# Engine orders from a list schedule, four shared PSUM slots, 1/x from its own activation table, and half-tile silu in a codec kernel

## Chip, cores, metric

One core of one Trainium2 chip. The metric is the device time of one execution in microseconds, lower is better; "median" is the median of the runs of one kernel. Engines: PE (matmul), DVE (VectorE), ACT (ScalarE), POOL (GpSimd), SP (issues the input DMAs).

## The reference

x is [2, 16000, 512] in bf16. A three-tap filter along time and a silu, four stages of residual quantization with a codebook of eight vectors each, and a three-tap filter over the chosen vectors:

```
z = silu(sum_i xp[:, i:i+T, :] * dw_enc[i])          # 3 taps, xp padded in time
res, q = z, 0
for s in range(4):
    d2  = |res|^2 - 2 * res . codebooks[s] + |codebooks[s]|^2
    sel = codebooks[s][argmin(d2)]
    q, res = q + sel, res - sel
y = sum_i qp[:, i:i+T, :] * dw_dec[i]                # 3 taps, qp padded in time
```

## The kernel before

A tile is 14 groups of 128 rows (1792 columns per channel block of 128 channels; there are four such blocks). A tile passes through *front* (taps and silu on DVE and ACT), *select* (products with the codebooks on PE, then a chain of small DVE steps that picks the vectors of stages 0 to 2), *resid* (24 updates of z through PSUM, then stage 3), and *back* (decode on PE, copies on ACT, store). Eighteen tiles, several in flight. The program only emits the steps in a rough order; the framework's own scheduler then orders each engine's instructions.

```python
psA = ctx.enter_context(tc.tile_pool(name="psA", bufs=3, space=bass.MemoryType.PSUM))  # 2 banks each
psS = ctx.enter_context(tc.tile_pool(name="psS", bufs=2, space=bass.MemoryType.PSUM))  # 1 bank each
...
def taps(st, i):                      # one channel block
    for k in range(K):
        t = ppool.tile([P, R], BF16, name=f"P{k}")
        nc.vector.tensor_scalar(out=t, in0=X[:, i, k:k + G, :]..., scalar1=WENC[:, i, k:k + 1], ... op0=ALU.mult)
    nc.vector.tensor_tensor(out=pk[0], in0=pk[0], in1=pk[1], op=ALU.add)
    nc.vector.tensor_tensor(out=pk[0], in0=pk[0], in1=pk[2], op=ALU.add)
    nc.scalar.activation(pk[1], pk[0], ACT.Exp, scale=-1.0)
def plus1(st, i):
    nc.vector.tensor_scalar(out=pk[1], in0=pk[1], scalar1=1.0, scalar2=None, op0=ALU.add)
    nc.scalar.activation(LN, pk[1], ACT.Ln)                    # 1/x = exp(-ln x), one table set
    nc.scalar.activation(pk[1], LN, ACT.Exp, scale=-1.0)
def gate(st, i): ...                  # z = tap sum * 1/(1 + exp(-tap sum))
...
def decide(st, s):                    # each step needs the result of the one before
    ... RC = pC + S; TR = cast(rr); PR = RC - CCF
    V = PR + TR; KEY = V + CCB; M = min(KEY); OH = (KEY == M)
def correct(st, s):                   # OT = copy of transposed OH; E2 = RC * OH; RD = sum(E2); rr += RD; pC = matmul
...
for _, _, f in sorted(order, key=lambda t: t[:2]):
    f()
```

Of the kernel before, what the change touches and what calls it, by code (L numbers as in the profile page):

```python
# [8 lines left out]
BF16 = mybir.dt.bfloat16  # L9
# [6 lines left out]

@with_exitstack
def kernel(
# [8 lines left out]





# [7 lines left out]
    G = 14  # L39
    GH = G // 2  # L40
    GC = G * C
    R = G * P
# [3 lines left out]
    assert T >= R  # L46
# [5 lines left out]
    ppool = ctx.enter_context(tc.tile_pool(name="ppool", bufs=3))  # L52
    lpool = ctx.enter_context(tc.tile_pool(name="lpool", bufs=2))
    selp = ctx.enter_context(tc.tile_pool(name="selp", bufs=2))
    small = ctx.enter_context(tc.tile_pool(name="small", bufs=3))
    ypool = ctx.enter_context(tc.tile_pool(name="ypool", bufs=2))
    psA = ctx.enter_context(tc.tile_pool(name="psA", bufs=3, space=bass.MemoryType.PSUM))
    psS = ctx.enter_context(tc.tile_pool(name="psS", bufs=2, space=bass.MemoryType.PSUM))


    nc.scalar.preload_act_table_set("natural_log_exp_and_others")


    IDENT = const.tile([P, P], BF16, name="IDENT")
    make_identity(nc, IDENT)
    ONES = const.tile([P, P], BF16, name="ONES")
    nc.vector.memset(ONES, 1.0)

    BIG = float(2.0 ** 100)
    MSK = const.tile([P, 3, ZW], BF16, name="MSK")  # L70
    nc.gpsimd.memset(MSK, 0.0)
    for u in range(3):
        nc.vector.tensor_scalar(out=MSK[:, u, N3:N3 + P], in0=IDENT, scalar1=BIG, scalar2=-BIG,
                                op0=ALU.mult, op1=ALU.add)

    WENC_b = const.tile([P, KT, K], BF16, name="WENC_b")
    WDBC = const.tile([P, K, D], BF16, name="WDBC")

    CB4 = const.tile([P, D], BF16, name="CB4")
    CB1 = const.tile([NC, D], BF16, name="CB1")  # L80
    wd_rows = bass.AP(tensor=dw_dec.tensor, offset=dw_dec.offset, ap=[[0, P], [D, K], [1, D]])
    with nc.allow_non_contiguous_dma(reason="small weights"):
        for k in range(K):
            nc.scalar.dma_start(out=WENC_b[:, :, k], in_=dw_enc[k].rearrange("(i p) -> p i", p=P))
        nc.scalar.dma_start(out=CB1, in_=codebooks.flatten_outer_dims())
        for s in range(Nq):
            for j in range(4):
                nc.scalar.dma_start(out=CB4[NC * s + C * j:NC * s + C * (j + 1), :], in_=codebooks[s])
        nc.scalar.dma_start(out=WDBC, in_=wd_rows)
    WENC = const.tile([P, KT, K], F32, name="WENC")  # L90
    nc.vector.tensor_copy(WENC, WENC_b)


    CBT = const.tile([P, KT, NC], BF16, name="CBT")
    CBM2 = const.tile([P, KT, NC], BF16, name="CBM2")
    for i in range(KT):
        pt = psS.tile([P, 512], F32, name="pt", tag="pss")
        ptb = pt.bitcast(BF16)[:, 0:NC]
        nc.tensor.transpose(ptb, CB1[:, i * P:(i + 1) * P], IDENT[0:NC, 0:NC])
        nc.vector.tensor_copy(CBT[:, i, :], ptb)  # L100
        nc.vector.tensor_scalar(out=CBM2[:, i, :], in0=ptb, scalar1=-2.0, scalar2=None, op0=ALU.mult)


    NZ = 3
    ZB = [const.tile([P, KT, G, ZW], BF16, name=f"ZB{b}") for b in range(NZ)]
    for b in range(NZ):
        for i in range(KT):
            nc.vector.tensor_copy(ZB[b][:, i, :, 0:N3], CBM2[:, i:i + 1, 0:N3].to_broadcast([P, G, N3]))
            nc.vector.tensor_copy(ZB[b][:, i, :, N3 + P:ZW], CBM2[:, i:i + 1, N3:NC].to_broadcast([P, G, C]))


    NX = 2
    XT = [const.tile([P, KT, G + 2, P], BF16, name=f"XT{b}") for b in range(NX)]
    for b in range(NX):
        nc.gpsimd.memset(XT[b][:, :, 0, 0:2], 0.0)
        nc.gpsimd.memset(XT[b][:, :, G + 1, P - 2:P], 0.0)


    pg = psS.tile([P, 512], F32, name="pg", tag="pss")
    for i in range(KT):  # L120
        nc.tensor.matmul(pg[0:NC, 0:NC], lhsT=CBT[:, i, :], rhs=CBT[:, i, :],
                         start=(i == 0), stop=(i == KT - 1))
    GR = const.tile([NC, NC], F32, name="GR")
    nc.vector.tensor_copy(GR, pg[0:NC, 0:NC])
    NPART = 3
    GP = const.tile([NC, NPART, NC], BF16, name="GP")
    GREM = const.tile([NC, NC], F32, name="GREM")
    nc.vector.tensor_copy(GP[:, 0, :], GR)
    nc.vector.tensor_tensor(out=GREM, in0=GR, in1=GP[:, 0, :], op=ALU.subtract)
    nc.vector.tensor_copy(GP[:, 1, :], GREM)  # L130
    nc.vector.tensor_tensor(out=GREM, in0=GREM, in1=GP[:, 1, :], op=ALU.subtract)
    nc.vector.tensor_copy(GP[:, 2, :], GREM)


    CCF = const.tile([P, 1, NC], F32, name="CCF")
    CCB = const.tile([P, 1, NC], BF16, name="CCB")
    CCD = const.tile([NC, NPART, NC], BF16, name="CCD")
    nc.vector.tensor_tensor(out=CCD, in0=GP, in1=IDENT[0:NC, 0:NC].rearrange("p (o c) -> p o c", o=1).to_broadcast([NC, NPART, NC]),
                            op=ALU.mult)
    pc = psS.tile([P, 512], F32, name="pc", tag="pss")  # L140
    for q in range(NPART):
        nc.tensor.matmul(pc[:, 0:NC], lhsT=ONES[0:NC, :], rhs=CCD[:, q, :], start=(q == 0), stop=(q == NPART - 1))
    nc.vector.tensor_copy(CCF[:, 0, :], pc[:, 0:NC])
    nc.vector.tensor_copy(CCB[:, 0, :], pc[:, 0:NC])



    GM = const.tile([GC, G, 1], F32, name="GM")
    nc.vector.tensor_reduce(out=GM[:, :, 0], in_=IDENT[0:GC, 0:GC].rearrange("p (g c) -> p g c", c=C), axis=AX.X, op=ALU.add)
    BD = {}  # L150
    for s in range(2):
        SEL = const.tile([NC, G, C], BF16, name=f"SEL{s}")
        nc.vector.tensor_copy(SEL, IDENT[0:NC, s * C:(s + 1) * C].rearrange("p (o c) -> p o c", o=1).to_broadcast([NC, G, C]))
        RP = const.tile([GC, NPART, NC], F32, name=f"RP{s}")
        pr = psS.tile([P, 512], F32, name="pr", tag="pss")
        nc.tensor.matmul(pr[0:GC, 0:NPART * NC], lhsT=SEL.rearrange("p g c -> p (g c)"),
                         rhs=GP.rearrange("p q c -> p (q c)"), start=True, stop=True)
        nc.vector.tensor_scalar(out=RP.rearrange("p q c -> p (q c)"), in0=pr[0:GC, 0:NPART * NC], scalar1=2.0,
                                scalar2=None, op0=ALU.mult)
        for s2 in range(s + 1, 3):  # L160
            for q in range(NPART):
                t = const.tile([GC, G, C], BF16, name=f"BD{s}_{s2}_{q}")
                nc.vector.tensor_tensor(out=t, in0=RP[:, q:q + 1, s2 * C:(s2 + 1) * C].to_broadcast([GC, G, C]),
                                        in1=GM.to_broadcast([GC, G, C]), op=ALU.mult)
                BD[s, s2, q] = t


    JM, SM = [], []
    idv = IDENT.rearrange("p (s j c) -> p s j c", s=Nq, c=C)
    for j in range(4):  # L170
        t = const.tile([P, 1], F32, name=f"JM{j}")
        nc.vector.tensor_reduce(out=t, in_=idv[:, :, j, :], axis=AX.XY, op=ALU.add)
        JM.append(t)


    WDEC = []
    for v, tp in enumerate(((0, 1, 2, None), (None, 0, 1, 2), (None, None, 0, None), (None, 2, None, None))):
        w = const.tile([P, D], BF16, name=f"WDEC{v}")
        acc = None
        for j, k in enumerate(tp):  # L180
            if k is None:
                continue
            t = const.tile([P, D], BF16, name=f"WJ{j % 2}")
            nc.vector.tensor_scalar(out=t, in0=WDBC[:, k, :], scalar1=JM[j], scalar2=None, op0=ALU.mult)
            if acc is not None:
                nc.vector.tensor_tensor(out=t, in0=t, in1=acc, op=ALU.add)
            acc = t
        nc.vector.tensor_tensor(out=w, in0=CB4, in1=acc, op=ALU.mult)
        WDEC.append(w)

    CBN = {}
    for s in range(3):
        for u in range(2):
            w = const.tile([P, D], BF16, name=f"CBN{s}_{u}")
            nc.gpsimd.memset(w, 0.0)
            r = slice(NC * s, NC * (s + 1))
            nc.vector.tensor_scalar(out=w[r, :], in0=CB4[r, :], scalar1=JM[1 + u][r, :], scalar2=-1.0,
                                    op0=ALU.mult, op1=ALU.mult)
            CBN[s, u] = w

    NOH = 4
    PADC = 2
# [3 lines left out]
    for t in OHA + OHW:  # L206
        nc.gpsimd.memset(t, 0.0)
    for t in KEY:
        k16 = t.bitcast(U16).rearrange("p g (c h) -> p g c h", h=2)
        for c in range(C):  # L210
            nc.gpsimd.memset(k16[:, :, c, 0], c)
# [290 lines left out]
```

## Time and profile before

| | before |
|---|---|
| median of 3 runs | 888.39 us (888.04 to 888.79) |
| DVE, ACT, PE busy | 739.6, 736.1, 631.2 us |
| steady stretch, 200 to 700 us: DVE, ACT, PE busy | 90%, 92%, 79% |
| distance of two tiles in the steady stretch | 44.3 us |
| first tap on DVE | 39.2 us |

The distance of two tiles is worked out from the starts of DVE's window copy (OHW, 96x896) of the 5th and the 16th tile, divided by 11.

The page of the kernel before, its line of engines and its chain that ended last (the work followed back from the last instruction to what released each piece):

```profile
PE 631.2 (71%) x4660; PEld 358.7 (40%) x4711; DVE 739.6 (83%) x1526; ACT 736.1 (83%) x667; POOL 79.7 (9%) x143
...
DVE 39%; ACT 29%; PE 22%; issue 5%; SPq 3%; DMA 1%; ACTq 0%; POOL 0%; POOLq 0%; DVEq 0%
```

The windows view of the kernel before, one stretch: its length, then busy time and instructions of each engine, the granted PE clock, the DMA share and GB/s:

```profile
core 0: us, PE busy (x) PEld busy (x) DVE busy (x) ACT busy (x) POOL busy (x), PEclk, DMA share, GB/s
200.00:700.00 500.00, 395.16 (x2926) 224.36 (x2958) 449.19 (x898) 460.61 (x420) 44.32 (x64) 0.92 0.39 81
```

No engine is full, and the chain wanders between three of them. The timeline of the kernel before. Columns: start, duration (both us), engine, line, operation, out<-in, shapes. The setup, where DVE waits for a weight before the first tap:

```profile
34.87 0.35 DVE L184 TENSOR_SCALAR WJ_235<-WDBC,JM_226 128x512 bf16<-128x512 bf16 x1 [13.77 <-DMA WDBC<-in_dw_dec_dram]
...
39.17 1.03 DVE L237 TENSOR_SCALAR P_346<-XT_164,WENC 128x1792 bf16<-128x1792 bf16 x1
```

Then a stretch of the small selection steps, on DVE alone:

```profile
402.22 0.27 DVE L319 TENSOR_TENSOR V<-PR,TR 128x112 bf16<-128x112 bf16 x1
402.40 0.27 DVE L319 TENSOR_TENSOR V<-PR_3825,rr_3826 128x112 bf16<-128x112 bf16 x1
402.59 0.28 DVE L322 TENSOR_TENSOR KEY_288<-V,CCB 128x112 bf16<-128x112 bf16 x1
402.77 0.28 DVE L322 TENSOR_TENSOR KEY_289<-V,CCB 128x112 bf16<-128x112 bf16 x1
402.96 0.26 DVE L324 TENSOR_REDUCE M<-KEY_288 128x14 f32<-128x112 f32 x1
403.14 0.26 DVE L324 TENSOR_REDUCE M<-KEY_289 128x14 f32<-128x112 f32 x1
```

Read the starts, not the durations: each step lasts 0.27 us, but the next one starts 0.18 us after it. The framework's scheduler has woven two selection chains (KEY_288 and KEY_289) into each other, so that a step never needs the result of the one just before it.

### The profile page before, as it was taken

The page shows a single profiled execution, that of the slowest core. Times are in us where ns is not written, and L with a number is a line of the kernel's source. Part 1 is how long each engine was busy: PE and PEld are TensorE (multiplying, and loading weights), DVE is VectorE, ACT ScalarE, POOL GpSimd, SP SyncE. Part 2 cuts the span into 40 slices and gives each one's busy share as a digit, 9 for nine tenths or more (in the row PEclk, how much of TensorE's full clock was granted, in tenths as well). Part 3 has the DMA queues.
Part 4 walks back from the last instruction along what each step waited for, and adds up shares of the span by engine and source line. Part 5 has one row for each costly group of instructions (what it writes and reads, how often), then busy time and mean ns, then how long its engine had stood idle before and what let it go on. Part 6 is the DMA issues. An engine that isn't in the chain of part 4 may idle for free.

```text
span 888.2 us, 12372 instructions
## 1 busy us (share of the span) xinstructions
PE 631.2 (71%) x4660; PEld 358.7 (40%) x4711; DVE 739.6 (83%) x1526; ACT 736.1 (83%) x667; POOL 79.7 (9%) x143
## 2 busy tenths in 40 slices
PE   1003587878787877777878787878787878778892
PEld 0002253535353535353535353535353535444540
DVE  4499999898989898989898989898989898984731
ACT  0076797989898989898989898989898989997572
POOL 5000000101010101010101010101010100000000
PEclk9998698989898989898989898989898989999997
DMA  4412322343434343434343534333534342020213
GB/s 96 95 30 59 78 46 39 94 74 92 75 94 73 96 71 97 70 100 67 99 68 99 68 97 66 103 65 100 67 99 67 98 69 78 7 84 1 84 51 112
DMA packets 143021, 67.20 MB, mean 76 GB/s; under 512 B 139932, under 2 KB 140572, under 8 KB 140700
## 3 DMA queue, kind: packets, MB, share of 16 engines
q1 hardware_dynamic: 137088, 33.06, 21.7%
q0 software_dynamic: 3840, 32.77, 11.8%
q10 hardware_dynamic: 2032, 0.56, 0.3%
q8 instruction: 37, 0.61, 0.3%
q14 instruction: 24, 0.20, 0.1%
HBM read 0.56 MB, written 32.77 MB: 38 GB/s over the span
## 4 chain that ended last, share of the span: by engine, by line
DVE 39%; ACT 29%; PE 22%; issue 5%; SPq 3%; DMA 1%; ACTq 0%; POOL 0%; POOLq 0%; DVEq 0%
PE pu L380 9%; PE pu L379 7%; ACT ZB_139 L384 6%; ACT ZB_137 L384 5%; ACT Y L402 5%; ACT ZB_138 L384 5%; SPq L228 3%; DVE ZB_137 L255 2%; DVE ZB_138 L255 2%; DVE ZB_139 L255 2%; PE pgr L270 2%; PE py L397 2%; DVE M L324 1%; DVE ZB_138 L386 1%; DVE ZB_139 L386 1%
## 5 line engine op out<-in xcount | busy, mean ns | idle before, releaser
L402 ACT CAST Y<-py 128x1024 bf16<-128x1024 f32 x126 | 130.6, 1043 | 13.8 <-PE py L397 13.8
L384 ACT CAST ZB_138<-pu 128x896 bf16<-128x896 f32 x108 | 95.9, 932 | 18.5 <-PE pu L380 18.0
L384 ACT CAST ZB_139<-pu 128x896 bf16<-128x896 f32 x108 | 95.6, 933 | 17.2 <-PE pu L380 16.7
L384 ACT CAST ZB_137<-pu 128x896 bf16<-128x896 f32 x108 | 95.7, 935 | 10.5 <-PE pu L380 10.5
L379 PEld LDWEIGHTS <-IDENT 128*128 128x128 bf16 x648 | 65.6, 101 | 77.8 <-issue 18.9
L270 PE MATMUL pgr<-ZB_137 128*128 128x152 bf16 (+1 forms) x672 | 56.4, 232 | 50.7 <-DVE ZB_137 L255 47.7
L379 PE MATMUL pu<-ZB_137,IDENT 128*128 128x512 bf16 (+1 forms) x216 | 81.1, 375 | 9.3 <-ACT ZB_137 L384 8.2
L379 PE MATMUL pu<-ZB_138,IDENT 128*128 128x512 bf16 x216 | 80.6, 373 | 7.8 <-ACT ZB_138 L384 6.7
L379 PE MATMUL pu<-ZB_139,IDENT 128*128 128x512 bf16 x216 | 80.1, 371 | 8.3 <-ACT ZB_139 L384 7.0
L267 PE MATMUL pgr<-MSK,IDENT 128*128 128x456 bf16 (+3 forms) x180 | 61.0, 339 | 23.2 <-ACT ZB_137 L384 4.8
L270 PEld LDWEIGHTS <-ZB_137 128*128 128x128 bf16 x672 | 48.4, 101 | 70.3 <-DVE ZB_137 L255 52.3
L288 DVE TENSOR_REDUCE rr<-pgr 128x6 f32<-128x768 f32 (+1 forms) x54 | 41.9, 775 | 36.2 <-PE pgr L270 36.1
L425 POOL DMA_DIRECT2D out_dram<-Y x66 | 34.1, 521 | 389.6 <-ACT Y L402 389.3
L386 DVE TENSOR_TENSOR ZB_139<-ZB_139,pu 128x896 bf16<-128x896 bf16 x36 | 39.1, 1085 | 27.9 <-PE pu L380 27.7
L386 DVE TENSOR_TENSOR ZB_138<-ZB_138,pu 128x896 bf16<-128x896 bf16 x36 | 39.0, 1083 | 20.5 <-PE pu L380 20.2
L270 PE MATMUL pgr<-ZB_139 128*128 128x152 bf16 (+1 forms) x672 | 53.3, 226 | 3.0 <-ACT ZB_139 L384 2.9
L270 PE MATMUL pgr<-ZB_138 128*128 128x152 bf16 (+1 forms) x672 | 53.6, 226 | 2.5 <-ACT ZB_138 L384 2.5
L270 PEld LDWEIGHTS <-ZB_139 128*128 128x128 bf16 x672 | 46.6, 98 | 18.4 <-issue 9.1
L270 PEld LDWEIGHTS <-ZB_138 128*128 128x128 bf16 x672 | 46.6, 98 | 17.7 <-issue 8.9
L386 DVE TENSOR_TENSOR ZB_137<-ZB_137,pu 128x896 bf16<-128x896 bf16 x36 | 39.0, 1084 | 12.1 <-PE pu L380 11.8
L242 ACT ACTIVATE P_348<-P_346 128x1792 bf16<-128x1792 bf16 x1 | 1.7, 1696 | 43.6 <-DVE P_346 L241 43.6
L380 PEld LDWEIGHTS <-CBN_0_262 128*128 128x128 bf16 x144 | 18.9, 131 | 32.6 <-issue 25.3
(1280 smaller groups left out, 1741.0 us busy)
## 6 DMA issues: line engine op xcount, KB each, us to landing
out_dram<-Y POOLq DMA_DIRECT2D x18, 1568.0 KB, 8.5
out_dram<-Y POOLq DMA_DIRECT2D x14, 196.0 KB, 8.2
XT_164<-in_x_dram SPq DMA_TRANSPOSE x126
XT_165<-in_x_dram SPq DMA_TRANSPOSE x126
out_dram<-Y POOLq DMA_DIRECT2D x30, 12.0 KB, 2.1
out_dram<-Y POOLq DMA_DIRECT2D x2, 210.0 KB, 8.9
WDBC<-in_dw_dec_dram ACTq DMA_DIRECT2D x1, 384.0 KB
CB_94<-in_codebooks_dram ACTq DMA_DIRECT2D x16, 8.0 KB
```

Of the source, the lines that this page charges most:

```text
L228: nc.sync.dma_start_transpose(out=X[:, :, g + 1, :], in_=src[g])
L255: nc.vector.tensor_tensor(out=Z[:, i, :, N3:N3 + P], in0=pk[0].rearrange("p (g c) -> p g c", c=P), in1=pk[1].rearrange("p (g c) -> p g c", ...
L267: nc.tensor.matmul(o, lhsT=IDENT, rhs=MSK[:, 0:nb, c0:c1], start=True, stop=False)
L270: nc.tensor.matmul(o[:, u * w:(u + 1) * w], lhsT=Z[:, i, b0 + u, N3:N3 + P], rhs=Z[:, i, b0 + u, c0:c1], start=False, stop=(u == nb - 1 an ...
L288: nc.vector.tensor_reduce(out=grp(st["rr"], g0, g1)[:, :, :, 0], in_=v[:, :, :, N3:N3 + P], axis=AX.X, op=ALU.max)
L379: nc.tensor.matmul(o, lhsT=IDENT, rhs=zg[:, k0:k0 + nk, :], start=True, stop=False)
L380: nc.tensor.matmul(o, lhsT=CBN[s, u][:, i * P:(i + 1) * P], rhs=W[:, k0:k0 + nk, PADC:PADC + P], start=not on_act, stop=True)
L384: nc.scalar.copy(zg, v)
L386: nc.vector.tensor_tensor(out=zg, in0=zg, in1=v, op=ALU.add)
L397: nc.tensor.matmul(o, lhsT=W[:, k, PADC:PADC + P], rhs=WDEC[u], start=True, stop=not wrap)
L402: nc.scalar.copy(Y[:, 2 * k:2 * k + 2, :].rearrange("p g d -> p (g d)"), py)
L425: nc.gpsimd.dma_start(out=view[p0:p1, lo:hi, :], in_=Y[p0:p1, lo:hi, :])
```

## The change

Its intent: give every engine a good fixed order. The program no longer emits instructions as it goes. It records steps with an engine, an estimated cost, a priority and their dependences; a greedy list schedule inside the kernel (at each turn the step that can start earliest, priority second) orders them, and manual scheduling keeps that order. With it:

- all PSUM use goes through four shared slots of two banks; at most two (QUOTA) may be held for one destination engine;
- 1/(1+e) comes from ACT's Reciprocal, which needs another table set than Exp, instead of Ln and Exp; the two halves of a tile (two channel blocks, 3584 columns) go through silu together, and a token forces the order Exp, Exp, Reciprocal, Reciprocal;
- the first tiles of one batch and the last of the other are small (6 and 8 groups): 20 tiles, the same number of groups;
- a few small DVE steps are dropped; the setup loads fewer pieces and moves some work to ACT.

The core of the diff, much cut:

```diff
+class Plan:
+    QUOTA = 2
+    LATENCY = {"PE": 0.26, "ACT": 0.2, "DVE": 0.13, "POOL": 0.25, "SP": 0.1, "DMA": 0.05}
 ...
+            for u in users[n]:
+                lat = self.LATENCY[s["e"]] if steps[u]["e"] != s["e"] else s["tail"]
+                at[u] = max(at[u], t + c + (s["tail"] if steps[u]["e"] != s["e"] else 0.0) + lat)
 ...
-    G = 14
+    SIZES = ([6, 8] + [14] * 8, [14] * 8 + [8, 6])
+    NA = 4
+    ON_DVE = (3, 7, 11, 15, 19, 23)
 ...
-    psA = ctx.enter_context(tc.tile_pool(name="psA", bufs=3, space=bass.MemoryType.PSUM))
-    psS = ctx.enter_context(tc.tile_pool(name="psS", bufs=2, space=bass.MemoryType.PSUM))
+    PS = [psum.tile([P, 1024], F32, name=f"ps{b}") for b in range(NA)]
 ...
-        nc.scalar.activation(LN, pk[1], ACT.Ln)
-        nc.scalar.activation(pk[1], LN, ACT.Exp, scale=-1.0)
+        add("ACT", act(2 * R), key(base + 0.5), lambda: recip(p1, p1), [], [..., "ACTTAB"], hold="R")
 ...
-    for _, _, f in sorted(order, key=lambda t: t[:2]):
-        f()
+    with tc.manual_schedule():
+        for s in plan.order():
+            s["fn"]()
```

## The prediction

> **What bounds the kernel now.** The page: DVE 739.6 us (83%), ACT 736.1 (83%), PE 631.2 (71%) of 888.2. In the windows from 200 to 800 us DVE is busy 90%, ACT 92 to 93%, PE 79%: no engine is full. The timeline of the DMA queue starts a tile load every 44.37 us; 18 x 44.37 = 799, so about 89 us are fill and drain. One tile costs DVE about 40 us, ACT about 41; the period is 44.4 because engines take turns. The chain of waits is mixed (DVE 39%, ACT 29%, PE 22%, issue 5%), passing through PSUM slots (PE pu, ACT ZB, PE pu).
>
> **Fill and drain.** Timeline: DVE stands 13.8 us behind the DMA of WDBC; the first tap runs at 39.2 us although the first tile's loads were issued by 19. From 840 us on DVE works 11 of 48 us.
>
> **What the change does**
> - Silu, ACT: 12 activations of 1792 columns per tile (every 1.60 us, 19.2 us) become 4 of 3584, about 3.08 each (estimate: 1.49 us of elements doubled, fixed 0.1 once), 12.3 us. Exp and Reciprocal need different tables; the order token forces Exp, Exp, Reciprocal, Reciprocal: two loads a tile. The trace's one load took 1.28 us: +2.6. The Trainium skill, "ScalarE: Activation LUTs", "What ACT_TABLE_LOAD costs", adds a drain of about 1.38 us per switch; this trace can't show it; the plan doesn't count it. ACT falls from about 41 to 36.5 without drain, 39 with.
> - DVE: taps, adds, 6 updates, evacuations unchanged. Merged halves and dropped small steps save about 0.6 us: about 39.4. DVE becomes the bound.
> - PE: same matmuls, about 35 us a tile.
> - PSUM: 3 double-bank plus 2 single-bank slots become 4 shared, at most 2 held for ACT. With two, a copy (0.80 us) and PE's refill (about 0.76 us plus two semaphore hops) make about 1.03 us per copy in a stretch of updates: ACT won't fill.
> - Tiles: 18 of 14 groups become 16 of 14 and two each of 6 and 8; same work, two more sets of fixed costs (estimate: 10 us DVE, 9 us ACT with tables).
> - Setup: no DVE queue behind WDBC, 16 small codebook DMAs gone, some work moved to ACT; the first load is 6 groups (1.3 us each), so taps start near 12 us. Tail: the last tile is 6 groups; DVE idles about 25 to 30 us there instead of about 40.
>
> **Sum.** Nearly all of it lies on the path. DVE work 739.6 - 9 - 5 + 10 = about 736; start and tail idle about 50; in steady state 4 to 5% idle (period 41 to 42), about 30. Total 816 us, 8% faster; 784 to 848 eight times in ten. Faster by over 2%: 0.92; within 2%: 0.05; slower: 0.03.
>
> **What would show it.** Period of loads 41 to 42; DVE 94 to 97% in the steady windows, ACT below 92%; about 40 table loads of 1.28 us, and gaps beside them if a drain is paid; first tap near 12 us; DVE total about 736, PE about 630, ACT 660 to 700.
>
> **What would make it wrong.** The order is fixed from estimated costs: where they are off (drain, semaphore hops, PE clock), engines wait in a wrong order and the period stays at 44. Four slots may be too few. If the plan fits well, the period is 40 and the time below 790.

## The result, and the profile after

| | before | after |
|---|---|---|
| median of 4 runs | 888.21 us | 872.32 us (871.59 to 874.66) |
| DVE, ACT, PE busy | 739.6, 736.1, 631.2 us | 784.2, 678.7, 625.1 us |
| 200 to 700 us: DVE, ACT, PE | 90%, 92%, 79% | 95%, 83%, 77% |
| distance of two tiles | 44.3 us | 44.0 us |
| first tap | 39.2 us | 25.0 us |
| DVE pairs, next step needs the one just before | 38 | 571 |
| DVE steps that start 0.02 to 0.05 us after the end of the one before | 85 | 597 |

The ratio is 0.9832 (95% interval 0.9815 to 0.9848): 1.7% faster, where I had said 8%. Ratios here are the mean time of one kernel's fast runs over that of the other kernel's of the same rounds, so not quite the ratio of the medians quoted. All outputs are right. The row of pairs counts neighbours in DVE's order, as the programs build it, of which the second reads the buffer that the first has just written. The expectations below give 70 for the kernel before: that count went by the names in the trace, where different buffers can share a name (by names the changed kernel has 612); by buffers it is 38. The last row is read from the traces alone; most other steps of both kernels start about 0.08 us before the end of the one before.

The page of the changed kernel, the same two lines:

```profile
PE 625.1 (72%) x4685; PEld 371.6 (43%) x4739; DVE 784.2 (90%) x1518; ACT 678.7 (78%) x636; POOL 98.1 (11%) x193
...
DVE 69%; PE 18%; issue 9%; ACT 2%; DVEq 0%; DMA 0%; POOL 0%; POOLq 0%; ACTq 0%; SPq 0%
```

The windows view of the changed kernel, the same stretch:

```profile
200.00:700.00 500.00, 383.37 (x2943) 233.50 (x2975) 476.23 (x864) 415.95 (x349) 54.24 (x90) 0.89 0.38 85
```

ACT lost 57 us, as planned. DVE is now the bound (95%, and 69% of the chain), as I had said. But its busy time *rose* by 45 us, with eight instructions fewer. The tiles follow each other no faster than before. From the first to the last tap on DVE the changed kernel even takes 4 us more (751.1 against 746.8); the 16 us gained lie before the first tap (14.2) and after the last (5.4). In the timeline of the changed kernel on DVE the selection steps stand like this:

```profile
423.42 0.27 DVE L244 TENSOR_TENSOR PR<-S,CCF 128x112 bf16<-128x112 f32 x1
423.73 0.27 DVE L244 TENSOR_TENSOR V<-PR,TR 128x112 bf16<-128x112 bf16 x1
424.04 0.28 DVE L244 TENSOR_TENSOR KEY<-V,CCB 128x112 bf16<-128x112 bf16 x1
424.36 0.27 DVE L502 TENSOR_REDUCE M<-KEY 128x14 f32<-128x112 f32 x1
424.66 0.28 DVE L244 TENSOR_TENSOR OHA<-KEY,M 128x112 bf16<-128x112 f32 x1
424.97 0.27 DVE L244 TENSOR_TENSOR E<-S,OHA 128x112 f32<-128x112 f32 x1
425.28 0.27 DVE L528 TENSOR_REDUCE RD<-E 128x14 f32<-128x112 f32 x1
```

The durations are those of before (0.27 us), but the starts are 0.31 us apart instead of 0.18: every step from the second on reads what the one before has written. Of the extra 0.12 us some 0.09 is lost overlap, which the view counts as busy, and some 0.03 is a gap, too short to be printed as a wait. So the mean durations of groups in the profile hardly show it (the V steps 0.27 us before, 0.29 after), and neither does a list of waits; only the distance of starts does.

Summed over the kernel, DVE's busy time plus its gaps of up to 0.06 us went from 742.8 to 804.5 us, by 62: by 8 before the first tap (14.1 to 22.2) and by 53.5 from there on (728.8 to 782.3). The 533 additional pairs at 0.123 us (measured alone below) are 66. That is enough for the whole rise after the first tap; by difference the rest of DVE's work there became some 10 us shorter, which I did not itemize.

The start of the changed kernel on DVE: three small copies last 9.4 us while POOL's memsets run, and the first tap comes at 25.0 us:

```profile
1.53 9.42 DVE L319 COPY SEL<-IDENT 32x112 bf16<-32x112 bf16 x2
1.72 9.27 DVE L334 COPY ROW<-IDENT 32x128 bf16<-32x128 bf16 x1
...
24.99 0.75 DVE L393 TENSOR_SCALAR P<-XT,WENC 128x768 bf16<-128x768 bf16 x2 [0.28 <-issue]
```

And ACT's table loads in the timeline of the changed kernel:

```profile
426.48 1.01 ACT L638 CAST YB<-ps 128x1024 bf16<-128x1024 f32 x1
427.51 1.28 ACT L423 ACT_TABLE_LOAD   x1
428.81 6.27 ACT L423 ACTIVATE P<-P 128x3584 bf16<-128x3584 bf16 x2
435.10 1.28 ACT L403 ACT_TABLE_LOAD   x1
436.39 3.19 ACT L403 ACTIVATE P<-P 128x3584 bf16<-128x3584 bf16 x1
```

There are 40 loads of 1.28 us. In the median a load starts 18 ns after the instruction before ends, and the next instruction 11 ns after the load: no drain of 1.38 us stands beside them.

### The profile page after: what moved, and what is told of

It reads as the page before. It is cut to its first block, busy times and chain, and to the rows that moved or that the text cites. A ratio compares the mean times of both kernels' runs of the same rounds, so it can differ in the third digit from the quotient of the medians.

```text
span 872.9 us, 12775 instructions
## 1 busy us (share of the span) xinstructions
PE 625.1 (72%) x4685; PEld 371.6 (43%) x4739; DVE 784.2 (90%) x1518; ACT 678.7 (78%) x636; POOL 98.1 (11%) x193
## 3 DMA queue, kind: packets, MB, share of 16 engines
q1 hardware_dynamic: 137088, 33.06, 19.7%
## 4 chain that ended last, share of the span: by engine, by line
DVE 69%; PE 18%; issue 9%; ACT 2%; DVEq 0%; DMA 0%; POOL 0%; POOLq 0%; ACTq 0%; SPq 0%
DVE P L393 12%; DVE P L244 11%; DVE ZB L580 11%; DVE ZB L244 5%; PE ps L572 5%; PE ps L571 4%; PE ps L437 4%; DVE rr L473 4%; DVE P L405 3%; DVE rr L596 3%; DVE KEY L244 2%; DVE V L244 2%; DVE OHA L244 2%; PE ps L630 2%; DVE M L502 2%
## 5 line engine op out<-in xcount | busy, mean ns | idle before, releaser
L578 ACT CAST ZB<-ps 128x896 bf16<-128x896 f32 (+2 forms) x360 | 285.3, 870 | 40.8 <-PE ps L572 38.5
L572 PE MATMUL ps<-OHW,CBN 128*128 128x512 bf16 (+1 forms) x864 | 293.0, 373 | 13.7 <-DVE ZB L580 10.0
L571 PE MATMUL ps<-ZB,IDENT 128*128 128x512 bf16 (+1 forms) x648 | 242.8, 375 | 28.6 <-DVE ZB L580 17.2
L437 PE MATMUL ps<-ZB 128*128 128x136 bf16 (+1 forms) x2016 | 164.3, 232 | 36.6 <-DVE ZB L244 32.4
L638 ACT CAST YB<-ps 128x1024 bf16<-128x1024 f32 x126 | 130.5, 1046 | 70.2 <-PE ps L630 66.1
L437 PEld LDWEIGHTS <-ZB 128*128 128x128 bf16 x2016 | 144.8, 100 | 78.8 <-DVE ZB L244 34.3
L244 DVE TENSOR_TENSOR P<-P,P 128x1792 bf16<-128x1792 bf16 (+2 forms) x160 | 160.3, 1002 | 3.5
L403 ACT ACTIVATE P<-P 128x3584 bf16<-128x3584 bf16 (+2 forms) x40 | 116.2, 2906 | 46.1 <-DVE P L244 45.9
L393 DVE TENSOR_SCALAR P<-XT,WENC 128x1792 bf16<-128x1792 bf16 (+2 forms) x240 | 150.4, 648 | 0.7 <-issue 0.5
L580 DVE TENSOR_TENSOR ZB<-ZB,ps 128x896 bf16<-128x896 bf16 (+2 forms) x120 | 117.6, 988 | 27.1 <-PE ps L572 26.7
L423 ACT ACTIVATE P<-P 128x3584 bf16<-128x3584 bf16 (+2 forms) x40 | 114.9, 2892 | 12.1 <-DVE P L405 11.9
```

Of the source, the lines that this page charges most:

```text
L244: add("DVE", cost, key, lambda: nc.vector.tensor_tensor(out=out, in0=a, in1=b, op=op), reads, writes, **kw)
L393: return lambda: nc.vector.tensor_scalar(out=dst, in0=X[:, i, k:k + G, :].rearrange("p g c -> p (g c)"), scalar1=WENC[:, k, i:i + 1], scal ...
L403: add("ACT", act(2 * R), key(base + 0.05), lambda: nc.scalar.activation(p1, p0, ACT.Exp, scale=-1.0), [("P0", sl, 0), ("P0", sl, 1)], [("P ...
L423: nc.scalar.add_instruction(mybir.InstActivation(name=nc.get_next_instruction_name(), engine=mybir.EngineType.Activation, func=ACT.Reciprocal,
L437: nc.tensor.matmul(o[:, u * w:(u + 1) * w], lhsT=Z[:, i, b0 + u, N3:N3 + P], rhs=Z[:, i, b0 + u, c0:c1], start=False, stop=(u == nb - 1 an ...
L571: nc.tensor.matmul(o, lhsT=IDENT, rhs=zg[:, k0:k0 + nk, :], start=True, stop=False)
```

## Experiments

Theory A: a DVE step that follows right behind the step whose result it needs costs about 0.12 us more. The plan does not know it, made over 500 more such pairs than the framework's scheduler, and spent there what it gained. Rivals: B, the fixed costs of two more tiles; C, four slots, two per engine, are too few; D, the table loads cost more than Ln did.

### e1: the DVE latency in the plan

```diff
-                lat = self.LATENCY[s["e"]] if steps[u]["e"] != s["e"] else s["tail"]
+                lat = self.LATENCY[s["e"]] if steps[u]["e"] != s["e"] else max(s["tail"], 0.12 if s["e"] == "DVE" else 0.0)
```

> The changed kernel, with one number put into its list schedule: a DVE step that needs the result of the DVE step before is ready 0.12 us after it, not at once. The same instructions in another order. Adjacent dependent DVE pairs fall from 571 to 135 (70 in the kernel before). Theory A (each such pair costs DVE about 0.12 us, the plan makes 500 more of them, and DVE became the bound): DVE work and its small gaps fall by about 50 us, busy from 784 to about 735, time 815 to 845. Theory B (two more tiles' fixed costs), C (four slots, two for ACT, are too few), D (table loads eat the silu gain): the time stays within 1% of 872.

Measured: 815.63 us (813.45 to 815.85), ratio 0.9183 to the kernel before (0.9161 to 0.9204). The page and the windows view of this version:

```profile
PE 607.8 (75%) x4693; PEld 369.8 (45%) x4739; DVE 736.0 (90%) x1518; ACT 675.4 (83%) x636; POOL 118.8 (15%) x193
...
DVE 52%; PE 27%; ACT 9%; issue 7%; DMA 2%; SPq 1%; DVEq 0%; ACTq 0%; POOL 0%; POOLq 0%
```

```profile
200.00:700.00 500.00, 407.83 (x3200) 251.68 (x3231) 484.65 (x919) 451.18 (x386) 70.49 (x96) 0.92 0.36 85
```

Its timeline on DVE shows why: a big step that is ready stands between two steps of the chain, and the next start comes 0.18 us after a small step:

```profile
433.81 0.27 DVE L244 TENSOR_TENSOR PR<-S,CCF 128x112 bf16<-128x112 f32 x1
433.99 1.09 DVE L244 TENSOR_TENSOR P<-P,P 128x1792 bf16<-128x1792 bf16 x1
434.99 0.27 DVE L244 TENSOR_TENSOR V<-PR,TR 128x112 bf16<-128x112 bf16 x1
435.18 0.68 DVE L393 TENSOR_SCALAR P<-XT,WENC 128x1792 bf16<-128x1792 bf16 x1
435.77 0.28 DVE L244 TENSOR_TENSOR KEY<-V,CCB 128x112 bf16<-128x112 bf16 x1
```

One number in the plan, and 57 us are gone: tiles follow every 40.3 us. DVE's busy time with small gaps fell from 804.5 to 741.1, by 63: by 57 from the first tap on (782.3 to 725.1), where the 436 pairs fewer are 54, and by 6 before it (22.2 to 16.1). There the copies take 0.51 instead of 9.42 us, but other setup steps take longer than in the changed kernel. So up to 6 of the 57 us may belong to the start (the first tap came 5.3 us earlier), not to the pairs.

### e10: a control, the same latency elsewhere

```diff
-                lat = self.LATENCY[s["e"]] if steps[u]["e"] != s["e"] else s["tail"]
+                lat = self.LATENCY[s["e"]] if steps[u]["e"] != s["e"] else max(s["tail"], 0.12 if s["e"] in ("ACT", "PE") else 0.0)
```

> A control: the changed kernel, with the same 0.12 us of own-engine latency put into the plan for ACT and PE instead of DVE. The plan's orders move about as much as with the DVE latency (2265 against 2732 lines of the DVE order differ from the change's, 1164 against 1128 on ACT), but the adjacent dependent DVE pairs stay at 586 (571 in the change, 135 with the DVE latency). Theory A: DVE busy stays at 775 to 790 us and the time within 1.5% of 872. If any other order of the plan is as good, it falls to 850 or below.

Measured: 875.48 us (871.86 to 879.05), ratio 0.9842. The page's line of engines:

```profile
PE 629.9 (72%) x4686; PEld 372.7 (42%) x4739; DVE 782.7 (89%) x1518; ACT 679.6 (77%) x636; POOL 103.7 (12%) x193
```

Its first tap came at 20.7 us, nearly as early as in e1, and its three copies took 0.51 us as in e1, and still it is not faster than the change: so the early start is not what made e1 fast, and this other order, with 586 pairs, isn't faster as such. Two more orders say the same: e3 and e4 below, where 614 and 608 DVE steps start 0.02 to 0.05 us after the one before (597 in the change, 149 in e1), stand at 879 and 882 us.

### m1: the pair alone

Behind the end of the changed kernel's program:

```diff
+        for _ in range(60):
+            t2(V0, I0)                 # V0 += I0, each on the result of the one before
+        for _ in range(30):
+            t2(V0, I0); t2(V1, I0)     # alternating
+        ...                            # the same 20 and 20 with 1792 columns, then tensor_scalar
```

> The changed kernel with a measuring block after its end (it changes no output, only the time): DVE adds of 112 bf16 columns, 60 each on the result of the one before, then 60 alternating over two tiles; the same 20 and 20 with 1792 columns; then 20 and 20 tensor_scalar steps of 1792 columns. Theory A: a step that waits for the one before starts about 0.30 us after it at 112 columns, one that alternates about 0.18; at 1792 columns about 1.12 against 1.00, and 0.65 against 0.54: the same 0.12 us whatever the size. If dependence costs nothing, both halves of each go at one pace.

The windows view of that run, inside four of the six stretches (count steps per length; 56 in 14 us are 0.250 us each, 56 in 7 us 0.125):

```profile
857.00:871.00 14.00, 3.12 (x8) 0.84 (x6) 12.10 (x56) 2.94 (x3) 1.01 (x2) 0.50 0.16 49
872.00:879.00 7.00, 0.00 (x0) 0.00 (x0) 7.00 (x56) 0.00 (x0) 0.00 (x0) 0.50 0.00 1
880.00:900.00 20.00, 0.00 (x0) 0.00 (x0) 19.39 (x19) 0.00 (x0) 0.00 (x0) 0.50 0.00 0
902.00:921.00 19.00, 0.00 (x0) 0.00 (x0) 19.00 (x20) 0.00 (x0) 0.00 (x0) 0.50 0.00 0
```

From start to start in the trace: 0.250 against 0.127 us at 112 columns, 1.126 against 1.002 at 1792, 0.661 against 0.536 for tensor_scalar. Dependence costs 0.123 to 0.125 us at both sizes. My absolute numbers at 112 columns were too high (perhaps because operands are plain here and broadcast in the kernel; not tested); the difference was right. In both halves nearly every step (193 of the 200 in all) carries a wait for DVE's own semaphore, by the trace; so the wait as an instruction is not the cost, but that it is not yet fulfilled. Whether a dependent step without that semaphore would be as slow can't be tried: it would be a race.

### b1: the kernel before in program order

```diff
-    for _, _, f in sorted(order, key=lambda t: t[:2]):
-        f()
+    with tc.manual_schedule():
+        for _, _, f in sorted(order, key=lambda t: t[:2]):
+            f()
```

> The kernel before with its instructions kept in the order in which its program gives them (manual scheduling, nothing else changed): adjacent dependent DVE pairs rise from 70 to 422. Theory A: DVE busy rises by about 352 x 0.12 = 42 us from 740 to about 780, and the time to 915 or more. Rival (the cost belongs to something in the new kernel, half tiles or shared slots, not to the order): DVE busy stays within 10 us of 740.

Measured: 1218.68 us, ratio 1.3717. DVE busy rose to 770.3; with small gaps from 742.8 to 785.3, by 42.5. I had expected 42 from 352 pairs, counted from the wrong 70; the 384 that there are would be 47 at 0.123 us. The effect is there in the old kernel too, without shared slots, plan or half tiles. Most of the 330 us is another thing: DVE's longer gaps grew from 126 to 412 us, presumably since in this order the engines wait for each other more (not traced further; PE's granted clock was lower too, 0.82 against 0.92). The framework's scheduler had been worth that much, silently.

### e2: eighteen tiles in the changed kernel

```diff
-    SIZES = ([6, 8] + [14] * 8, [14] * 8 + [8, 6])
+    SIZES = ([14] * 9, [14] * 9)
```

> The changed kernel with the tiles of the kernel before: 18 of 14 groups instead of 16 of 14 and two each of 6 and 8. 514 adjacent dependent DVE pairs instead of 571. Theory B (fixed costs of two more tiles ate the gain): DVE busy falls by 15 us or more and the time falls below 862. Theory A: DVE work falls by about 12 us, but fill and drain of a 14-group tile come back, so the time is 872 to 890.

Measured: 861.45 us, ratio 0.9708, DVE busy 763.0. Faster, against what I expected from theory A. Theory B's numbers are met (DVE's busy time fell by 21 us). Counted from the first tap on, busy time with small gaps fell by 17 us (782.3 to 765.0); 57 pairs fewer are 7 of them. That leaves about 10 us for the fixed costs of two tiles, what I had put into my sum: the small tiles cost about what was foreseen, so they don't explain the miss. Nor are they a rival for the 57 us of e1, which keeps all 20 tiles.

### e7: eighteen tiles in the best version

The same edit, on the version of e6 below.

> The best version so far (0.12 us DVE latency in the plan, 5 updates on DVE, 796.6 us), with 18 tiles of 14 groups instead of 20 with small ones at both ends. In the kernel of the change the same edit gained 11 us, against my expectation. If the small tiles cost more than they save (their fixed costs and more dependent pairs), the time falls by 5 to 12 us here too. If that gain was an effect of the stalled DVE (57 fewer dependent pairs of 0.12 us are 7 us), the time stays within 4 us or rises, for a 14-group tile fills and drains longer.

Measured: 833.72 us, against 796.6 with the small tiles. Neither of my alternatives foresaw so much. DVE worked less (711.4 against 717.1 us) but its longer gaps grew from 56 to 93 us; the tiles follow at 31 and 52 us in turn, 42.6 in the mean. So the plan settled into a worse pattern in the steady part. From the last tap on DVE to the end it takes 124.9 us here against 99.2 in e6 (109.9 in e2 against 96.8 in the changed kernel): small last tiles make the end shorter. What they cost in between differs in sign between e2 and e7, with the plan's order, so their worth as a whole stays open.

### e3 and e9: three slots for one engine

```diff
-    QUOTA = 2
+    QUOTA = 3
```

> The changed kernel with up to 3 of the 4 PSUM slots held for one engine, in the plan, instead of 2. Theory C (ACT starves behind two slots): time below 860 and ACT's idle time behind PE down by a third. Theory A: within 1% of 872, for the order of small DVE steps is as bad (582 adjacent dependent pairs).

> The best version so far with up to 3 PSUM slots held for one engine in the plan instead of 2. If PSUM slots now bound it (DVE no longer stalled by its own order): 5 to 15 us faster than 796.6. If not: within 1%, or slower as in the kernel of the change (+7 us).

Measured: 879.28 us in the changed kernel (0.8% slower than it, by the medians) and 815.98 us in the version of e6 (796.6 without). Theory C falls in this form: more slots per engine don't help. In e9 the plan's order has 211 adjacent pairs instead of 82, and DVE is 10 us busier (727.3 against 717.1); this explains part of the loss.

### e4 and e5: 1/x by Ln and Exp again

```diff
-        add("ACT", act(2 * R), ..., lambda: recip(p1, p1), ..., hold="R")
+        add("ACT", act(2 * R), ..., lambda: nc.scalar.activation(p1, p1, ACT.Ln), ..., hold="E")
+        add("ACT", act(2 * R), ..., lambda: nc.scalar.activation(p1, p1, ACT.Exp, scale=-1.0), ..., hold="E")
```

In place, for there was no room for a float32 buffer.

> The changed kernel with 1/x computed as before, by Ln and Exp from one table set (in place, so bf16 between them, a little less exact), half tiles kept: 6 activations of 3584 columns per tile instead of 4, no table loads after the first. ACT busy rises by about 70 us (36 more half-tile activations of 3.1 us is 110, less 40 loads of 1.28 is 51, so about 60) from 679 to about 740. Theory A (ACT is off the path while DVE is at 95%): time within 1.5% of 872. If ACT were on the path the time would rise by 30 us or more. Theory D (the loads with a hidden drain cost more than Ln saves): the time falls.

> The version with 0.12 us of DVE latency in its plan (815.6 us), with 1/x by Ln and Exp again from one table, in place. ACT work per tile rises from about 36.5 to 40 us and becomes the larger. If ACT is now close to the path: the time rises by 25 to 60 us, to 840 to 875, more than the 10 us that the same edit cost in the kernel of the change. If DVE still hides it: within 1.5% of 816.

Measured: e4 882.05 us with ACT busy 738.3; e5 836.81 us with ACT busy 733.9. The change freed 60 us of ACT (738.3 to 678.7), but that was worth only 10 us in the changed kernel, and at most 21 us once DVE was free of its own order: e5's order is also worse for DVE, with 223 steps that start 0.02 to 0.05 us after the one before instead of 149 in e1 (at 0.12 us, 9 us), and DVE is 11 us busier (747.4 against 736.0). In e5 DVE and ACT are both at 94% in the stretch from 200 to 700 us. Theory D falls: with its table loads the reciprocal is the faster way in both. That e5 came out just below my range of 840 to 875 fits ACT being near the path there, not on it alone; since DVE's order changed too, it doesn't show it.

### e6 and e8: fewer updates on DVE

On top of e1:

```diff
-    ON_DVE = (3, 7, 11, 15, 19, 23)
+    ON_DVE = (3, 8, 13, 18, 23)        # e6
+    ON_DVE = (5, 11, 17, 23)           # e8
```

> The version with 0.12 us of DVE latency in its plan, with 5 instead of 6 of a tile's 24 residual updates on DVE and 19 on ACT. Theory A (DVE is the bound at 97% busy in the steady stretch): DVE loses 1.0 us a tile, 18 us in all, ACT gains 15; the time falls by 5 to 18 us from 816. If ACT or PE is the true bound the time stays or rises.

> The version with 0.12 us of DVE latency in its plan, with 4 instead of 6 of the updates on DVE (796.6 us with 5). DVE work per tile falls to about 37.3 us, ACT's rises to about 38.1: ACT would become the larger, and the plan's own order has 260 adjacent dependent DVE pairs again, against 82. Expected: no better than 5 on DVE, 795 to 825 us.

Measured: e6 796.56 us (795.09 to 798.66), ratio 0.8964 (0.894 to 0.8989): the best version, 10% faster than the kernel before and correct. The 19 us gained on e1 are just above the 5 to 18 that I expected, and not all belong to the moved update: this plan also has 82 adjacent pairs instead of 135, about 6 us. e8 816.71 us. The windows view of e6 in the steady stretch:

```profile
200.00:700.00 500.00, 431.28 (x3435) 262.83 (x3433) 480.40 (x954) 478.92 (x419) 68.72 (x101) 0.96 0.39 89
```

DVE and ACT are both at 96%, and tiles follow every 38.8 us. In e8 the plan brings 260 adjacent pairs back; DVE is 4 us busier than in e6 (721.1), although it has 20 updates fewer; the copies at its start took 9.4 us again, so that counted from the first tap on, with small gaps, it is 5 us (709.2 against 704.6).

## Why the prediction was wrong, point by point

- **The step that failed**, as put: "DVE: taps, adds, 6 updates, evacuations unchanged. Merged halves and dropped small steps save about 0.6 us: about 39.4", and in the sum "DVE work 739.6 - 9 - 5 + 10 = about 736". I costed DVE by kind and number of instructions and took their durations from a trace in which a good order hid a part of each. DVE came out at 784.2 us busy, plus 20 us of gaps under 0.06 us each (3 before). The runs showed in its place: 533 more neighbours of which the second needs the first, at 0.123 us 66 us; DVE's busy time with small gaps rose by 53.5 us from the first tap on, where my sum has all of DVE's work fall by 4. With the order mended (e1) DVE's busy time was 736.0 us and the median 815.6 us, what I had predicted for the change itself. The agreement to a microsecond is partly luck, for the start was off by 8 us.
- I had named orders made from wrong costs ("drain, semaphore hops, PE clock") as what could make me wrong, but not the latency inside one engine, which the diff states in one line as zero. The number could have been read before I predicted: small steps in the trace of before start 0.18 us apart and last 0.27.
- Right: DVE became the bound (95% in the steady stretch; I said 94 to 97%, but expected that share at a shorter distance of tiles). Wrong: that distance, 44.0 us instead of 41 to 42; it was 40.3 in e1.
- Right: ACT's total (678.7 us, said 660 to 700), 40 table loads of 1.28 us, PE's total (625, said 630). The drain I allowed for did not show in the trace.
- Wrong: the first tap near 12 us. It came at 25.0. Setup work of DVE stands in front, and in the profiled run the three small copies lasted 9.4 us. In e1 the first tap came at 19.7 us.
- "Nearly all of it lies on the path" was wrong for ACT's part in the changed kernel: 60 us of ACT were worth 10 us there (e4), at most 21 after the repair (e5).
- The two slots for ACT: I expected a loss. Three slots were no better, twice (e3, e9), so that reason for a full ACT being out of reach isn't shown.
- Open: what the small tiles are worth as a whole (e2 and e7 point opposite ways), and how much of the differences among e5 to e9 is the greedy plan's luck. A small edit moves its whole order.

## What to carry to other kernels

When a change takes the order of instructions away from a scheduler, the order is a cost of its own: compare distances of starts, not durations, and count neighbours that need each other's results. A list schedule has to know the latency within an engine as well as that between engines; here 0.12 us for DVE, put into one line, was worth 57 us of 872 (up to 6 of them perhaps from the start), and with one update fewer on DVE 76. Time taken from an engine that isn't the bound shows up only after the bound is gone, so try such a part again after each repair.

## What the Trainium skill lacked or had wrong

- "VectorE: DVE Perf Modes", section "The DRAIN you can't avoid", and its rule for chained DVE ops (the drain happens in any case, so mind the number of ops, not the semaphores): the section says that the next op waits until the pipe is empty, though one that is not held starts earlier. The runs show that the order matters: 0.250 us per step in a chain, 0.127 alternating over two tiles, and 0.124 us more per dependent step at 1792 columns too. That a semaphore costs nothing extra, as the section says of eight copies, agrees with the alternating half of `m1_pairs_alone`, which carries waits at 0.127 us per step; in the chained half, where each wait is not yet fulfilled, the runs show 0.123 us more.
- "Perfetto Trace Analysis", section "Optimizing Scalar/DVE Operations", says that the write-acknowledgement half of an instruction's latency overlaps with the next instruction. The trace agrees for independent steps (duration 0.204, distance 0.127 us); the section has no figure for a dependent step, which gets none of this overlap (duration 0.216, distance 0.250 us).
- "ScalarE: Activation LUTs", section "What ACT_TABLE_LOAD costs": the load's 1283 ns is what all 40 loads took. The drain of about 1380 ns beside it is not there: 18 ns before and 11 ns after, in the median; nor does it hide in the first activation after a load (3190 ns at 3584 columns, the others 3193).
- "ScalarE: Activation LUTs", section "What it computes", warns of ACT's Reciprocal for accuracy. The result passed against the reference in each run that used it, with bf16 around it.
- "SBUF — State Buffer", section "Terms", calls the port pair that DVE and GpSimd share an exclusive lock, held for one instruction. The three copies at the start could fit this, but they stood beside many POOL memsets, not one: 9.42 us in the changed kernel, 2.30 in `m1_pairs_alone` with the same program up to there, 0.51 in e1. How long DVE loses is not settled by the page nor by these runs; I did not isolate it.
